# Seven block products for eight in the value product of batches 4 to 7, accumulated in one bank with copies between

## Chip, cores and metric

One Trainium2 chip, one core. The metric is device time of one launch in microseconds (us), median of several executions. Kernel before: 342.56 us (342.53 to 343.09), as it stood when the prediction was made. A profile is one such execution; its span is some 2 us shorter than the time (339.4 us for 341.31 in the profile of the kernel before, 338.8 for 340.82 in that after). The profile of the kernel before is of an execution of 341.31 us, so of one faster than that median.

## The reference

Eight batches, eight heads, 576 tokens, head size 64, all float32. Linear attention without softmax, RMS norm per head, then a gated linear unit with a causal convolution of five taps as gate:

```
kv   = einsum('bhsd,bhse->bhde', k, v)
out  = einsum('bhsd,bhde->bhse', q, kv)
x    = out / sqrt(mean(out*out, -1) + 1e-6) * g_norm        # then heads side by side: (B, S, 512)
gate = sigmoid(sum over k of conv_w[k] * shifted(x, k))     # five taps, causal
val  = x @ w_val                                            # 576x512 by 512x512, per batch
y    = (gate * val) @ w_out
```

## The kernel before

The kernel writes down "steps" with an engine, a duration and needs; a planner puts them into one program order, shifted by a table of hand-found offsets (SHIFTS). So each change to a step or a buffer gives all five engines a new order. The parts that matter:

```python
BANKS = {"kv": 1, "raw": 2, "tp": 2, "mm": 3}        # PSUM banks; tp = transposes, mm = products

def val_product(b, jt, n):            # 128 output columns, 288 tokens; 8 of these per batch
    val = ps("mm", [P, SV], f"val{b}_{jt}_{n}")
    for kc in range(NK):              # NK = 4 blocks of the inner dimension
        nc.tensor.matmul(val[:], wval[:, kc, jt * P:(jt + 1) * P],
                         xTs[b % 3][:, kc, HALO + n * SV:HALO + (n + 1) * SV],
                         start=(kc == 0), stop=(kc == NK - 1))

def keep_val(b, jt, n): nc.scalar.copy(out=gv[...], in_=st["val", b, jt, n][:])     # ScalarE
def gate_tap(b, jt, tap): nc.vector.scalar_tensor_tensor(...)                       # VectorE, 4 per gate
def gate_end(b, jt): nc.scalar.activation(out=gate[:], in_=gate[:], func=AF.Sigmoid)  # ScalarE
def gated(b, jt): nc.vector.tensor_tensor(out=both, in0=both, in1=gate[:], op=ALU.mult)
def halo(b): ...                      # GpSimd, edge tokens of xT; waits for DMAs that move xT
def powers(b, c): ...                 # GpSimd, mean square -> 1/rms ("rt")
...                                   # cut: loads, weight conversion, attention, the planner
```

The output product (w_out) already used seven block products for eight in this kernel.

## Time and profile before

| | before |
|---|---|
| time | 342.56 us |
| profiled span, mean granted TensorE clock | 339.4 us, 0.995 |
| TensorE (PE) busy | 315.1 us, 93% |
| VectorE (DVE) busy | 270.4 us, 80% |
| ScalarE (ACT), GpSimd (POOL) busy | 139.4, 140.0 us |
| TensorE instructions | 2161, of them value product 512 |

How to read it: TensorE sets the time from about 42 us on (busy for 270.3 of the 272 us from 42 to 314); the columns "idle before" and "releaser" of a group or of the timeline say what ended a wait. One more measure is used throughout, and I work it out from the timeline: the **lag** of TensorE at an instruction is its start time less the work that stands before it in TensorE's queue, each kind counted at its issue interval of the undisturbed middle (value 0.2427 us, fast output 0.2158, attention 0.1117, small key-value products 0.0365). Where the lag grows, TensorE lost time, by idling or by running slower; where it stays level, nothing was lost. The kernel before has a lag of 15.5 us at work 91, 16.1 at work 180, 16.1 at work 290 and 18.8 at its last product: it loses next to nothing between 110 and 315 us. (How transposes are weighted isn't given. Redone from the traces with transposes counted as attention, single values move by up to 0.8 us from work 90 on and by up to 3 us before it, but differences between kernels by 0.5 at most; it is the differences that count below.)

### The profile page before, as it was taken

The numbers are of one execution on the slowest core, as the hardware profiler recorded it, in microseconds if no ns is written. First come the engines' busy times: TensorE is split into PE (matmuls) and PEld (weight loads), VectorE is DVE, ScalarE is ACT, GpSimd is POOL, SyncE is SP. The second block draws the span as 40 slices with busy tenths as digits, with TensorE's granted clock in tenths as the row PEclk, the third lists the DMA queues.
The fourth block names the chain that finished last, engine by engine and source line by source line (L and its number), as shares of the span: only waits on it lengthen the run. The fifth ranks groups of instructions, "written<-read, shape, count | busy, mean of one in ns | idle before, by whom it ended". The sixth has DMA issues, their size and how long they took to land.

```text
span 339.4 us, 6185 instructions
## 1 busy us (share of the span) xinstructions
PE 315.1 (93%) x2161; PEld 254.7 (75%) x2161; DVE 270.4 (80%) x496; ACT 139.4 (41%) x293; POOL 140.0 (41%) x178
## 2 busy tenths in 40 slices
PE   0858999999999999999999999999999999999794
PEld 0747777878778877788778888778878876878681
DVE  4607999989999799896999899789956997297620
ACT  5528983873134253235134533172215322353010
POOL 3007314784356642683365585601717458000000
PEclk9998999999999999999999999999999999999999
DMA  6999979997077979787793165365333215220223
GB/s 165 287 329 306 320 219 299 250 315 168 3 178 196 244 233 280 187 236 207 206 256 86 32 154 157 71 182 144 79 89 85 64 31 129 58 63 2 62 62 93
DMA packets 46012, 55.35 MB, mean 163 GB/s; under 512 B 15754, under 2 KB 36254, under 8 KB 45982
## 3 DMA queue, kind: packets, MB, share of 16 engines
q1 hardware_dynamic: 42750, 48.67, 52.7%
q0 software_dynamic: 3072, 6.30, 8.3%
q8 instruction: 17, 0.28, 0.4%
q14 instruction: 13, 0.11, 0.1%
q10 hardware_dynamic: 160, 0.00, 0.0%
HBM read 39.21 MB, written 9.44 MB: 143 GB/s over the span
## 4 chain that ended last, share of the span: by engine, by line
PE 77%; DVE 8%; DMA 8%; ACT 3%; SPq 2%; issue 1%; POOL 1%; DVEq 0%
PE val L567 34%; PE ac L639 15%; PE b L639 11%; PE raw L469 8%; DMA q<-in_q_dram 5%; PE kv L392 4%; DMA k<-in_k_dram 2%; PE out L587 2%; PE qTps L430 2%; DVE gate L555 2%; PE xTps L515 1%; DVE sums L622 1%; DVE gv L580 1%; DMA out_dram<-ot 1%; DVE ss L491 1%
## 5 line engine op out<-in xcount | busy, mean ns | idle before, releaser
L567 PE MATMUL val<-xT,wval 128*128 128x288 f32 x512 | 129.5, 407 | 0.5 <-ACT gv L576 0.5
L567 PEld LDWEIGHTS val<-xT,wval 128*128 128x128 f32 x512 | 95.8, 190 | 26.9 <-issue 1.5
L497 POOL TENSOR_TENSOR rt<-ss,mhalf 128x8 f32<-128x8 f32 (+1 forms) x40 | 66.5, 1668 | 114.7 <-DVE ss L491 114.4
L555 DVE SCALAR_TENSOR_TENSOR gate<-xT,cwT,gate 128x576 f32<-128x576 f32 x128 | 97.4, 808 | 1.9 <-ACT gate L549 1.9
L538 POOL DMA_DIRECT2D xT<-y x96 | 52.9, 557 | 18.1 <-issue 6.5
L576 ACT COPY gv<-val 128x288 f32<-128x288 f32 x64 | 25.3, 395 | 69.3 <-PE val L567 69.1
L469 PEld LDWEIGHTS raw<-kvbd,qT 128*128 128x128 f32 (+1 forms) x320 | 36.8, 187 | 5.0 <-issue 1.9
L469 PE MATMUL raw<-kvbd,qT 128*128 128x128 f32 (+1 forms) x320 | 40.1, 286 | 0.0
L491 DVE TENSOR_REDUCE ss<-sq 128x8 f32<-128x520 f32 (+1 forms) x40 | 25.0, 630 | 17.5 <-ACT sq L483 17.5
L639 PE MATMUL b<-wsum,sums 128*128 128x256 f32 x128 | 33.6, 385 | 3.1 <-DVE sums L622 2.7
L639 PE MATMUL ac<-wout,gv 128*128 128x256 f32 x128 | 33.6, 385 | 0.2 <-DVE ot L662 0.2
L483 ACT ACTIVATE sq<-raw 128x512 f32<-128x512 f32 (+1 forms) x40 | 22.0, 553 | 24.0 <-PE raw L469 23.9
L639 PEld LDWEIGHTS b<-wsum,sums 128*128 128x128 f32 x128 | 23.1, 190 | 7.7 <-DVE sums L622 2.3
L504 DVE TENSOR_TENSOR x<-raw,rt 128x512 f32<-128x512 f32 (+1 forms) x40 | 24.9, 627 | 3.0 <-POOL rt L497 2.7
L639 PEld LDWEIGHTS ac<-wout,gv 128*128 128x128 f32 x128 | 23.4, 190 | 4.7 <-DVE ot L662 1.1
L562 ACT ACTIVATE gate<-gate 128x576 f32<-128x576 f32 x32 | 21.6, 684 | 11.8 <-DVE gate L555 11.4
L580 DVE TENSOR_TENSOR gv<-gv,gate 128x576 f32<-128x576 f32 x32 | 24.0, 749 | 2.6 <-ACT gv L576 1.9
L545 POOL COPY xT<-xT 128x124 f32<-128x124 f32 x32 | 18.7, 622 | 13.5 <-DMA xT<-y 13.5
L549 ACT ACTIVATE gate<-xT,cwT 128x576 f32<-128x576 f32 x32 | 22.2, 765 | 2.3 <-DMA xT<-y 2.2
L392 PEld LDWEIGHTS kv<-v,k 128*64 128x64 f32 x512 | 17.8, 138 | 6.5 <-issue 5.7
L392 PE MATMUL kv<-v,k 128*64 128x64 f32 x512 | 20.4, 225 | 1.9 <-DMA v<-in_v_dram 1.9
L655 ACT COPY ot<-ac 128x256 f32<-128x256 f32 x16 | 6.0, 372 | 35.6 <-PE ac L639 30.1
(78 smaller groups left out, 335.1 us busy)
## 6 DMA issues: line engine op xcount, KB each, us to landing
q<-in_q_dram SPq DMA_DIRECT2D x96, 140.0 KB, 4.6
out_dram<-ot SPq DMA_DIRECT2D x144, 64.0 KB, 1.8
k<-in_k_dram SPq DMA_DIRECT2D x16, 512.0 KB, 8.0
v<-in_v_dram SPq DMA_DIRECT2D x16, 512.0 KB, 7.3
xT<-y POOLq DMA_DIRECT2D x96, 64.0 KB, 2.7
w_wval<-in_moe_w_val_dram SPq DMA_DIRECT2D x4, 512.0 KB, 7.0
q<-in_q_dram SPq DMA_DIRECT2D x4, 512.0 KB, 8.7
w_wout<-in_moe_w_out_dram SPq DMA_DIRECT2D x4, 512.0 KB, 8.6
```

The lines of the kernel that those rows point to most:

```text
L392: nc.tensor.matmul(kvp[r * D:(r + 1) * D, hp, :], st["k", b, half][:, h, j, :] if j < NJ else kl[:, 2 * hp + r, :], st["v", b, half][:, h, ...
L469: nc.tensor.matmul(raw[row * m:(row + 1) * m, col * P:(col + 1) * P], st["qT", b][:, hp, c * P:c * P + m], kv_bd[b % 2][:, hp, :], start=T ...
L491: nc.vector.reduce_sum(out=ss[:, 0:n], in_=st["sq", b, c][:, 0:n], axis=AX.X)
L497: nc.gpsimd.tensor_tensor(out=rt[:, 0:n], in0=st["ss", b, c][:, 0:n], in1=mhalf[:, 0:n], op=ALU.pow)
L504: nc.vector.tensor_tensor(out=x[:, 0:n * D].rearrange("p (h e) -> p h e", h=n), in0=st["raw", b, c][:, 0:n * D].rearrange("p (h e) -> p h ...
L538: nc.gpsimd.dma_start(out=xTs[b % 3][i * TB:(i + 1) * TB, :, first:first + P], in_=y[a * TB:(a + 1) * TB, i])
L549: nc.scalar.activation(out=gate[:], in_=xTs[b % 3][:, jt, HALO:SX], func=AF.Copy, scale=cwT[:, K - 1, jt:jt + 1])
L555: nc.vector.scalar_tensor_tensor(out=gate[:], in0=xTs[b % 3][:, jt, tap * TB:tap * TB + S], scalar=cwT[:, tap, jt:jt + 1], in1=gate[:], op ...
L567: nc.tensor.matmul(val[:], wval[:, kc, jt * P:(jt + 1) * P], xTs[b % 3][:, kc, HALO + n * SV:HALO + (n + 1) * SV], start=(kc == 0), stop=( ...
L576: nc.scalar.copy(out=gv[:, jt, first:first + SV], in_=st["val", b, jt, n][:])
L580: nc.vector.tensor_tensor(out=both, in0=both, in1=st["gate", b, jt][:], op=ALU.mult)
L639: nc.tensor.matmul(st[bank, i, p], tokens()[:, k], weights_[:, k], start=(n < 2 and k == 0), stop=(k == NK // 2 - 1), skip_group_check=True)
```

## The change

Intent: per batch, the value product is a 2x2 block product; with sums of blocks of x and of w_val beforehand it needs 7 block products for 8. Block products pile up in one bank: product 0, 2, 4 and 6 go into bank "a" one onto the other, and between them ScalarE or VectorE copies the intermediate state out. The core of the diff:

```diff
-    BANKS = {"kv": 1, "raw": 2, "tp": 2, "mm": 3}
+    BANKS = {"kv": 1, "raw": 2, "tp": 1, "mm": 4}
+    FAST_VAL = range(4, B)
+    GATES = 3                       # gate buffers, were 4; xT buffers 2, were 3 (comments added here)
+    def val_sums(n): ...            # 4 sums of value weights, once          (VectorE)
+    def x_sums(b, n): ...           # 4 differences of x per batch           (VectorE)
+    def val_fast(b, mj, n):
+        bank, weights_, tokens = (
+            ("a", wval[:, EVEN, cols(0)], block(EVEN, 0)), ("c", vsum[:, 0, :, cols(0)], total(0)),
+            ("a", vsum[:, 1, :, cols(0)], total(1)), ("b", wval[:, ODD, cols(0)], block(ODD, 0)),
+            ("a", vsum[:, 2, :, cols(0)], total(2)), ("c", vsum[:, 3, :, cols(0)], block(ODD, 1)),
+            ("a", wval[:, ODD, cols(1)], total(3)))[n]
+        for k in range(NK // 2):
+            nc.tensor.matmul(st[bank, "val", b, mj][:], weights_[:, k], tokens()[:, k],
+                start=(n in (0, 1, 3) and k == 0), stop=(k == NK // 2 - 1), skip_group_check=True)
+    def val_keep(b, mj, n):         # n 0,1,2,6: ScalarE copies; 3,4,5: VectorE adds into gv
+        ...
+    def out_bank(i, p):             # the last output pairs use attention's banks
+        return "raw" if i == B // 2 - 1 and p != 2 else "mm"
     def fast_product(i, p, n):      # output product: same bank scheme, 3 adds and 4 copies per pair
...                                  # cut: gates in order 0,2,1,3; weight conversions in the
...                                  #      output buffers (ot); planner entries
-SHIFTS = {...}                      # all offsets new: loads, weight conversions, attention, gates
+SHIFTS = {...}
```

## The prediction

> **What bounds the kernel now.** I read the page first (busy shares, slices), then the groups, then the chain that ended last in order of time, then the start on VectorE.
>
> ```profile
> PE 315.1 (93%) x2161; PEld 254.7 (75%) x2161; DVE 270.4 (80%) x496; ACT 139.4 (41%) x293; POOL 140.0 (41%) x178
> ...
> PE   0858999999999999999999999999999999999794
> ...
> DVE  4607999989999799896999899789956997297620
> ...
> DMA  6999979997077979787793165365333215220223
> ```
>
> TensorE (PE) is idle for 24.3 of 339.4 us. Tables by stretch place it: 15.5 us before 42 us (loads and the first attention), 1.7 between 42 and 300, 1.9 at about 317, some 5 in the last copy and store. In the middle nothing but TensorE work sets the time, so an instruction removed there is worth its issue interval, if nothing new waits. The chain in order of time (start, length) gives the intervals, the groups (busy, mean ns) the durations of the other engines:
>
> ```profile
> 195.94 13.58 PE val L567 x56
> 209.53 0.86 PE ac L639 x4
> ```
>
> ```profile
> L567 PE MATMUL val<-xT,wval 128*128 128x288 f32 x512 | 129.5, 407 | 0.5 <-ACT gv L576 0.5
> ...
> L576 ACT COPY gv<-val 128x288 f32<-128x288 f32 x64 | 25.3, 395 | 69.3 <-PE val L567 69.1
> ...
> L580 DVE TENSOR_TENSOR gv<-gv,gate 128x576 f32<-128x576 f32 x32 | 24.0, 749 | 2.6 <-ACT gv L576 1.9
> ...
> L655 ACT COPY ot<-ac 128x256 f32<-128x256 f32 x16 | 6.0, 372 | 35.6 <-PE ac L639 30.1
> ...
> L662 DVE TENSOR_TENSOR ot<-b,ot 128x256 f32<-128x256 f32 x16 | 6.7, 418 | 1.8 <-PE b L639 1.6
> ...
> L606 DVE TENSOR_TENSOR wsum<-wout 128x512 f32<-128x512 f32 x2 | 1.4, 677 | 0.0
> ```
>
> A value matmul shows as two instructions; 56 take 13.58 us, 0.2425 each[...]. A product of the fast output (4 instructions) takes 0.86.
>
> [...] 407 ns busy against 242 issued. I count intervals, not busy time. [...]
>
> **The change, part by part.**
> 1. Removed: batches 4 to 7 need 7 block products of 4 instructions in each of 2 column pairs, 56 where 64 were. That is 32 instructions x 0.2425 = **7.8 us**. My count over the whole order of instructions, each kind at its interval, gives 315.4 before and 307.7 after.
> 2. VectorE: 16 differences of x at 0.75 (12.0), 24 block adds at about 0.45 (10.8, scaled from 0.418 for 256 columns), 4 weight sums at 0.68 (2.7); the re-ordered output products use 3 adds for 5, which saves 32 x 0.418 = 13.4. Net **+12 us**, to about 282. To see whether it becomes the bound I set the sums of VectorE work and TensorE work side by side at each point where a product needs a sum. Before, the second batch's sums came just in time (the products wait at 109 us, and 104 to 109 of the chain is VectorE). After, that place has 3 us more VectorE work ahead, but one weight block is converted in the idle gap at 14 to 25 us, so it is about level. In the last four batches VectorE leads by 10 to 14 us. So it should not become the bound, though its reserve at the end shrinks from 27 us to about 13.
> 3. ScalarE: 8 copies per batch as before, and 4 for 2 in each output pair, 32 more x 0.37 = 12. It ends near 45%, off the path except through waits.
> 4. New waits. After product 0, a copy must end before product 2 goes into the same bank, with product 1 between; so again from 2 to 4 and 4 to 6. The trace has a copy start 0.26 us after the product's last issue, lasting 0.395 (add 0.45), and TensorE following 0.06 later: 0.72 against 0.97 of product 1. That fits, with little left to load the weights early (0.19). Before, 18 such waits had just one product between and cost under 1 us together. After, by the order, there are 37, 17 of them in the value product. Whenever ScalarE is in a 0.77 us gate start or VectorE in a 0.75 us tap, one slips. I take 0.04 us each: **+1.5 us**. One bank change (batch 6's first half to the next output) has no work between: **+0.8**.
> 5. The tail, from the same chain:
>
> ```profile
> 316.26 0.41 ACT gv L576
> ...
> 316.69 0.77 DVE gv L580
> ...
> 317.48 0.70 DVE sums L622
> ...
> 318.21 0.70 DVE sums L622
> ...
> 318.96 1.13 PE b L639 x4
> ```
>
> TensorE waits 1.87 us for copy, gating and two sums. The new product order needs one sum first (0.7 less), and two output products now lie beside the copy and gating where one did. The path after the last value product is 0.28 + 0.40 + 0.76 + 0.69 + 0.07 = 2.2 us, against 1.7 of products: about 0.5 is left, a gain of **1.3**. Attention's banks spare the last pairs a wait for a free bank, but their second output buffer is still held by its store, as before (0.24). The last copy and store stay.
> 6. The start, where the order of loads and the banks change too (transposes have one bank for two). The timeline of TensorE, then of VectorE:
>
> ```profile
> 24.41 6.05 PE L469 MATMUL raw<-kvbd,qT 128*64 128x128 f32 x40
> ...
> 38.27 0.63 PE L515 MATMUL xTps<-ident,x 128*128 128x128 f32 x4
> ```
>
> ```profile
> 25.53 0.42 DVE L491 TENSOR_REDUCE ss<-sq 128x4 f32<-128x260 f32 x1 [11.22 <-ACT sq L483]
> 26.45 0.43 DVE L327 TENSOR_SCALAR wexp_wval<-w_wval 128x512 uint32<-128x512 uint32 x1 [0.49 <-DMA w_wval<-in_moe_w_val_dram]
> ```
>
> Transfers limit this stretch (DMA share over 1 from 6 us on; 6.8 MB by 26 us). After, a value weight block and the next batch's small q come ahead of the last half of v: 0.66 MB more, so the first attention product starts at about 25.5 for 24.4. Two converting steps for output weights stand in VectorE's queue before and among the first sums; their data are 6.6 and 7.1 MB down the queue, an estimated 27.7 and 29.2 us. [...] the last x is ready at about 39.5 for 38.05, and TensorE reaches that transpose with 19.8 us of work done, not 21.4. Together about **+2.9 us**. Since TensorE is then later and VectorE is not, the small VectorE waits between 42 and 110 us (1.2 us) should go: **-1.2**.
>
> Sum: -7.8 - 1.3 + 1.5 + 0.8 + 2.9 - 1.2 = -5.1, so **337.5 us**.
>
> **Rivals.**
> A: all of the removed time is gained and the start costs nothing. TensorE is saturated from 42 to 314 us, and the skeleton of loads is near the same. 342.6 - 7.8 - 1.3 + 1 = 334.5. Against it: the two weight conversions in front of the first sums.
> B: a new wait takes the place of the removed work. Each value product now depends on ScalarE and VectorE every 0.97 us, where the former product ran 1.94 us alone with three free banks. With 0.15 us lost at each of 37 tight waits (a third of a busy engine's usual remainder) that is 5.6, not 1.5: 341.5. For it: VectorE is over 90% busy there. Against it: 18 tight waits before cost almost nothing, and the order was plainly tuned anew around them.
> C: VectorE becomes the bound of the last batches (reserve used up by gates with 3 buffers for 4, x with 2 for 3). Each 0.76 us step of lag appears in full at the output products: 342 to 345. The reserve of 10 us or more speaks against it.
>
> **Range and chances.** The removal is certain, the start is the largest doubt (0 to +4), then the tight waits (0.5 to 5). 80%: 334.0 to 341.0. Faster by over 2% means under 335.7: it needs the start to cost under 1 us or so, which I give 0.31. Slower by 2% needs C and B together: 0.03.
>
> **What would show it.** Right: value instructions 480, not 512, still 0.242 apart; VectorE about 282 us busy; idle of TensorE before 42 us up by 2 to 4; gap at the last sums under 0.8 us; TensorE waits on copies 1 to 3 us in total. Start wrong: the first x transposes done at 38 us with idle still 15.5. B right: TensorE (or its weight load) idle on the copies to gv and ot by 4 us or more. C right: several us idle on x differences, sums or gating after 190 us, with VectorE over 95% busy. Above 341 or under 334 my account of the waits is wrong.

## The result, and the profile after

The changed kernel took **340.88 us** (340.60 to 341.98, 4 runs), the kernel before on the same chip 342.82 (342.53 to 343.25, 4 runs). Ratios here are the mean time of one kernel's fast runs over that of the other's of the same rounds, so not quite the ratio of the quoted medians: 0.9948, 95% interval 0.9923 to 0.9974. Half a per cent faster, inside the predicted range, but little over a third of the predicted gain (1.9 us of 5.1). A second set of executions on another chip (after_again, below) gave 0.9973, so the two estimates of the gain are 1.8 and 0.9 us.

The head of the page after, to be set against the line of before in the prediction:

```profile
PE 312.4 (92%) x2129; PEld 250.4 (74%) x2129; DVE 281.3 (83%) x504; ACT 151.2 (45%) x325; POOL 139.6 (41%) x178
```

32 TensorE instructions fewer, VectorE at 281.3 us (predicted 282), ScalarE 12 more: the counted parts came out as counted. Now the table by stretch, before and then after; columns are start and end, length, busy time of TensorE, weight load, VectorE, ScalarE and GpSimd (with instructions), granted TensorE clock, DMA share and GB/s:

```profile
0.00:42.00 42.00, 26.55 (x349) 22.94 (x350) 23.37 (x64) 25.73 (x58) 11.72 (x19) 0.96 1.03 281
42.00:110.00 68.00, 66.69 (x586) 54.14 (x583) 66.14 (x118) 35.52 (x75) 34.31 (x32) 1.00 0.75 204
...
190.00:250.00 60.00, 60.00 (x341) 47.67 (x339) 54.83 (x93) 22.15 (x45) 28.72 (x43) 1.00 0.48 122
250.00:300.00 50.00, 50.00 (x237) 40.24 (x234) 34.82 (x59) 18.57 (x38) 21.70 (x29) 1.00 0.29 72
```

```profile
0.00:42.00 42.00, 23.35 (x290) 19.97 (x291) 25.27 (x64) 24.33 (x52) 11.74 (x19) 0.94 1.04 287
42.00:110.00 68.00, 68.00 (x553) 55.25 (x551) 65.18 (x116) 37.48 (x80) 24.30 (x26) 0.99 0.83 218
...
190.00:250.00 60.00, 58.30 (x393) 45.42 (x392) 55.40 (x97) 22.69 (x50) 32.95 (x44) 1.00 0.52 133
250.00:300.00 50.00, 49.36 (x224) 38.87 (x223) 45.38 (x76) 21.27 (x46) 21.77 (x29) 1.00 0.27 64
```

TensorE is idle 3.2 us more before 42 us, 1.3 less up to 110 us, and has gaps from 190 to 300 us where it had none. VectorE was 97% busy from 42 to 110 us before already, and is 96% after.

The lag, point by point (same work, both profiles):

| at | before | after | what the step adds |
|---|---|---|---|
| work 90 (about 106 and 110 us) | 15.5 | 20.5 | start: +5.0 |
| work 180 | 16.1 | 20.4 | middle: -0.7 |
| work 290 | 16.1 | 24.7 | batches 4 to 7: +4.3 |
| last product | 18.8 | 26.0 | tail: -1.4 |

Together +7.2, against 7.8 us of work removed: -0.6, which is the difference of the two spans (339.4 and 338.8). The timed gain was 1.9. The gap comes from the profile of before: its execution took 341.31 us, 1.5 less than the median of the timed ones (342.82), while that of after, 340.82, lay at its median, and a second profile of the changed kernel (after_again) has the same lag at work 90. Time and granted clock go together: in the set of runs of the kernel before that stood beside after_again, 14 executions at 0.992 or more have a median span of 338.75 us, 20 at 0.985 or less 341.4, which is 2.65 us (0.8%) more and over the whole gain of this change. Which of the two brings about the other isn't shown. So 1 to 2 us of the start's 5.0 belong to the execution profiled, not to the kernel: 1.3, if the timed gain is taken as the true sum.

**The start.** VectorE after, where the first sums of squares (ss) wait behind a converting step for the output weight and its data:

```profile
27.41 0.43 DVE L330 TENSOR_SCALAR wexp_wout<-w_wout 128x512 uint32<-128x512 uint32 x1 [0.79 <-DMA w_wout<-in_moe_w_out_dram]
27.76 0.42 DVE L494 TENSOR_REDUCE ss<-sq 128x4 f32<-128x260 f32 x1
```

The first sum came at 27.76 for 25.53, 1.6 us after ScalarE had done its squares (sq, from 25.77 for 0.39 us): it stood behind the converting step, which waited 0.79 us for its data, until 27.41. TensorE in the same stretch, before and then after:

```profile
36.03 2.11 PE L567 MATMUL val<-xT,wval 128*128 128x288 f32 x8
...
40.83 0.64 PE L392 MATMUL kv<-v,k 128*64 128x64 f32 x16
```

```profile
29.98 0.66 PE L525 MATMUL xTps<-ident,x 128*128 128x128 f32 x2 [2.28 <-ACT sq L486]
30.43 1.92 PE L472 MATMUL raw<-kvbd,qT 128*128 128x128 f32 x8
...
38.97 0.66 PE L525 MATMUL xTps<-ident,x 128*128 128x128 f32 x4 [2.20 <-ACT xT L532]
39.56 0.69 PE L395 MATMUL kv<-v,k 128*64 128x64 f32 x16
40.07 0.38 PE L395 MATMUL kv<-vl,kl 128*64 128x64 f32 x4
40.23 1.07 PE L395 MATMUL kv<-v,k 128*64 128x64 f32 x16
```

Two things are to be seen. A transposition of x stands ahead of ready attention work in TensorE's queue and waits 2.28 us; another waits 2.20 us for the one transpose bank. And after each wait the same instructions take longer in this profile: 8 attention instructions (at 30.43 us) 1.92 us for 1.06, 16 key-value products (at 40.23 us) 1.07 us for 0.64, the first 8 value instructions (at 42.36 us) 2.69 for 2.11. The granted clock was 0.74 from 28 to 32 us and 0.57 from 40 to 44 us in this execution; in the one profiled for after_again, with waits of 2.28 and 2.31 us at the same places, it was 1.00 and 0.73. In the kernel before it was 0.64 from 24 to 28 us, after a wait of 1.89 us. What sets it isn't shown.

**The late batches.** The largest stall, at 216 us, read downwards through four engines (GpSimd, VectorE, ScalarE, TensorE):

```profile
211.06 1.16 POOL L555 COPY xT<-xT 128x124 f32<-128x124 f32 x4 [5.72 <-DMA xT<-y]
212.20 1.03 POOL L500 TENSOR_TENSOR rt<-ss,mhalf 128x4 f32<-128x4 f32 x1
```

```profile
213.26 0.42 DVE L515 TENSOR_TENSOR x<-raw,rt 128x256 f32<-128x256 f32 x1 [1.89 <-POOL rt L500]
213.61 1.54 DVE L565 SCALAR_TENSOR_TENSOR gate<-xT,cwT,gate 128x576 f32<-128x576 f32 x2
```

```profile
215.18 0.68 ACT L572 ACTIVATE gate<-gate 128x576 f32<-128x576 f32 x1 [2.01 <-DVE gate L565]
215.77 0.35 ACT L723 COPY ot<-cb 128x256 f32<-128x256 f32 x1
```

```profile
216.18 1.13 PE L710 MATMUL cb<-wout,gv 128*128 128x256 f32 x4 [1.47 <-ACT ot L723]
...
276.80 1.13 PE L710 MATMUL cb<-wout,gv 128*128 128x256 f32 x4 [0.42 <-ACT ot L723]
278.95 1.13 PE L710 MATMUL cb<-wout,sums 128*128 128x256 f32 x4 [0.16 <-DVE ot L719]
```

GpSimd's halo of batch 5 waits for a DMA (5.72 us), the powers of batch 6 stand behind it, VectorE's normalising waits for them (1.89 us), gate taps of batch 4 stand behind that, ScalarE's sigmoid waits for the taps (2.01 us), the copy of a finished bank stands behind the sigmoid, and TensorE waits for the copy (1.47 us). The product that is copied at 215.77 had ended at 213.6. The lag rises by 1.4 there, 0.4 at 230.8, 0.6 at 276.8 and 0.3 at 279.0 us: 2.7 of 4.3; the rest comes in steps of 0.1 to 0.2, mostly where one kind of product follows another. All four are waits of an output product for the copy or addition that must come between two products in one bank.

The tail is as predicted: the wait at the last sums is short.

```profile
318.18 1.13 PE L710 MATMUL cb<-wsum,sums 128*128 128x256 f32 x4 [0.28 <-DVE sums L687]
```

### The profile page after: what moved, and what is told of

The parts are those of the page before. It is cut to its first block, busy times and chain, and to the rows that moved or that the text cites. A ratio compares the mean times of both kernels' runs of the same rounds, so it can differ in the third digit from the quotient of the medians.

```text
span 338.8 us, 6161 instructions
## 1 busy us (share of the span) xinstructions
PE 312.4 (92%) x2129; PEld 250.4 (74%) x2129; DVE 281.3 (83%) x504; ACT 151.2 (45%) x325; POOL 139.6 (41%) x178
## 4 chain that ended last, share of the span: by engine, by line
PE 69%; DMA 10%; DVE 10%; SPq 4%; issue 3%; ACT 2%; DVEq 0%
PE val L577 19%; PE a L710 12%; PE cb L710 11%; PE raw L472 7%; PE va L627 6%; DMA q<-in_q_dram 6%; PE kv L395 5%; PE vc L627 3%; DMA w_wout<-in_moe_w_out_dram 2%; SPq L739 2%; PE out L655 2%; PE qTps L433 2%; DVE gate L565 2%; DVE ot L719 2%; DMA kl<-in_k_dram 1%
## 5 line engine op out<-in xcount | busy, mean ns | idle before, releaser
L500 POOL TENSOR_TENSOR rt<-ss,mhalf 128x8 f32<-128x8 f32 (+1 forms) x40 | 68.2, 1706 | 109.4 <-DVE ss L494 109.2
L577 PE MATMUL val<-xT,wval 128*128 128x288 f32 x256 | 65.7, 410 | 0.0
L577 PEld LDWEIGHTS val<-xT,wval 128*128 128x128 f32 x256 | 48.2, 192 | 12.6 <-issue 0.3
L710 PE MATMUL a<-wsum,sums 128*128 128x256 f32 x128 | 33.3, 382 | 0.0
L494 DVE TENSOR_REDUCE ss<-sq 128x8 f32<-128x520 f32 (+1 forms) x40 | 25.2, 631 | 4.4 <-ACT sq L486 4.1
L719 DVE TENSOR_TENSOR ot<-cb,ot 128x256 f32<-128x256 f32 x32 | 13.4, 418 | 16.7 <-PE cb L710 8.0
L515 DVE TENSOR_TENSOR x<-raw,rt 128x512 f32<-128x512 f32 (+1 forms) x40 | 24.7, 620 | 2.5 <-POOL rt L500 2.5
L586 ACT COPY gv<-val 128x288 f32<-128x288 f32 x32 | 12.7, 400 | 30.8 <-PE val L577 30.8
L710 PEld LDWEIGHTS a<-wsum,sums 128*128 128x128 f32 x128 | 23.4, 190 | 3.3
L555 POOL COPY xT<-xT 128x124 f32<-128x124 f32 x32 | 16.4, 553 | 7.0 <-DMA xT<-y 5.9
L433 PE MATMUL qTps<-ident,q 128*64 128x128 f32 (+1 forms) x160 | 13.3, 319 | 6.5 <-DMA q<-in_q_dram 4.9
L710 PE MATMUL cb<-wout,gv 128*128 128x256 f32 x64 | 16.6, 382 | 1.9 <-ACT ot L723 1.9
```

The lines of the kernel that those rows point to most:

```text
L494: nc.vector.reduce_sum(out=ss[:, 0:n], in_=st["sq", b, c][:, 0:n], axis=AX.X)
L500: nc.gpsimd.tensor_tensor(out=rt[:, 0:n], in0=st["ss", b, c][:, 0:n], in1=mhalf[:, 0:n], op=ALU.pow)
L515: nc.vector.tensor_tensor(out=x[:, 0:n * D].rearrange("p (h e) -> p h e", h=n), in0=st["raw", b, c][:, 0:n * D].rearrange("p (h e) -> p h ...
L577: nc.tensor.matmul(val[:], wval[:, kc, jt * P:(jt + 1) * P], xTs[b % 2][:, kc, HALO + n * SV:HALO + (n + 1) * SV], start=(kc == 0), stop=( ...
L710: nc.tensor.matmul(st[bank, i, p], tokens()[:, k], weights_[:, k], start=(n < 2 and k == 0), stop=(k == NK // 2 - 1), skip_group_check=True)
```

## The experiments

Fifteen kernels ran, in four groups, each group on one chip beside the kernel before (341.3 to 342.4 us there, scattering by 4 to 5 us). Ratios are to the kernel before, from fast executions alone, with their 95% interval; times are medians of all.

### plain_val: eight products again, all else as changed

```diff
-    FAST_VAL = range(4, B)
+    FAST_VAL = range(B, B)
```

> The changed kernel with 8 value products again in batches 4 to 7 (nothing else undone); the order of instructions is the same up to 188 us. It adds 7.8 us of TensorE work after 188 us and takes 23 us of VectorE work and 32 copies between products away. Theory W (the new waits on VectorE and ScalarE in the last four batches cost about 4.4 us, as the lag of TensorE behind its work grew from 20.4 to 24.9 us between 206 and 310 us): 340.9 + 7.8 - 4.4 = 344.3. Rival H (all that is missing was lost in the start, the seven products gain their whole 7.8): 348.7.

Correct, 351.07 us, ratio 1.0256 (1.0212 to 1.0299): some 10 us over the changed kernel, above both theories and more than the 7.8 of the products: in this order there is also a wait of 3.61 us on VectorE before 263 us. So it doesn't say what the seven products are worth, nor does it part the costs.

### nowait_val: the copies between products wait for nothing

Result wrong on purpose: the copies after products 0, 1, 2 and the add after 4 read a weight in SBUF in place of the bank, so TensorE need not wait for them.

```diff
-            nc.scalar.copy(out=to(0, 0), in_=a)
+            nc.scalar.copy(out=to(0, 0), in_=other)      # other = wout[:, mj, 0:SV]; likewise n = 1, 2, 4
```

> Wrong result on purpose, same order of instructions: the copies after value products 0, 1, 2 and the add after 4 read a weight from SBUF and not the bank, so TensorE never waits for a copy between value products. Rival B (the tight waits inside the value product are the cost): 336.5 to 337.5. Theory V (the cost sits where VectorE is late, and shows at output products): 1 us or less gained, 339.9 to 340.9.

340.85 us, ratio 0.9975 (0.9953 to 0.9996), and the lag grows by 4.1 us from work 180 to 260, in the changed kernel by 4.3; TensorE's idle time from 190 to 300 us is 2.5 us (changed kernel 2.3). The time lies with the changed kernel's 0.9948 and 0.9973. The tight waits of the value product (copies of 0.40 us and adds of 0.45 between products of 0.97) cost nothing measurable. That takes away 17 of the 37 waits that the prediction had counted, not the 20 of the output product.

### short_taps: less VectorE work in the late gates

Result wrong on purpose: the gate taps of batches 4 to 7 on a quarter of the columns.

```diff
+        w = S // 4 if b in FAST_VAL else S
-            out=gate[:], in0=xTs[b % 2][:, jt, tap * TB:tap * TB + S],
+            out=gate[:, 0:w], in0=xTs[b % 2][:, jt, tap * TB:tap * TB + w],
```

> Wrong result on purpose, same order: the 64 taps of the gates of batches 4 to 7 run over a quarter of the columns, which takes about 64 x 0.45 = 29 us off VectorE and leaves every wait in place. Theory V (VectorE late in the last four batches, ScalarE's gate ends and the copies behind them with it): TensorE's stalls after 206 us go, 336.5 to 338. Rival B (tight waits themselves): within 1 us of 340.9.

The 0.45 us per tap is an estimate from the trace of the kernel before: a VectorE product or sum of two tensors takes 0.749 us over 576 columns (gv, L580) and 0.418 over 256 (ot, L662), so in proportion 432 columns fewer are worth about 0.45. 338.57 us, ratio 0.9901 (0.9863 to 0.9940). The product of the stall at 216:

```profile
215.21 1.13 PE L711 MATMUL cb<-wout,gv 128*128 128x256 f32 x4 [0.36 <-ACT ot L724]
```

There the lag steps up by 0.3 us for 1.4, at 277 to 279 by nothing over 0.3, and the lag grows by 1.8 from work 180 to 260 where it grew by 4.3. TensorE's idle time from 190 to 300 us falls from 2.3 to 0.7. So the larger part of the late loss came by way of VectorE being late.

### late_order: six steps put later, same work

Each step is taken out of the finished program order and put in again behind another (written short here):

```diff
+MOVES = [((halo, 5), after (powers, 6, 4)),
+    ((gate_end, 4, 1), after (fast_keep, 1, 3, 2)), ((gated, 4, 1), after (gate_end, 4, 1)),
+    ((gate_end, 6, 0), after (fast_keep, 2, 3, 1)), ((gate_end, 6, 2), after (fast_keep, 2, 3, 2)),
+    ((gated, 6, 2), after (fast_keep, 2, 3, 4))]
```

> The changed kernel with six steps of the batches 4 to 7 put later in the queues and nothing else: GpSimd's halo of batch 5 after the powers of batch 6, ScalarE's sigmoid of gates of batches 4 and 6 after the output copies that TensorE waits for. Queue theory: the stalls of TensorE at 216 (1.4 us) and at 277 to 279 us (0.9 together) go or shrink to 0.4 or less, the lag grows from work 180 to 300 by 2.5 to 3.5 us instead of 5, and the time falls by 0.4 to 0.7% against after_again. Rival (VectorE as a whole is short of time there, so that what is put later is missed later): the stall at 216 goes but returns at the next gating or output copy, lag at work 300 within 0.7 us of after_again's, time within 0.2%.

Correct, 339.36 us, ratio 0.9906 (0.9882 to 0.9930); the unaltered changed kernel beside it (after_again, below) 0.9973. GpSimd and TensorE in the place of the chain above:

```profile
210.02 1.47 POOL L510 TENSOR_TENSOR rt<-ss,mhalf 128x4 f32<-128x4 f32 x1 [1.84 <-DVE ss L504]
214.15 2.04 POOL L565 COPY xT<-xT 128x124 f32<-128x124 f32 x4 [2.65 <-DMA xT<-y]
```

```profile
217.16 0.38 PE L535 MATMUL xTps<-ident,x 128*128 128x128 f32 x2
217.38 1.03 PE L720 MATMUL cb<-wout,gv 128*128 128x256 f32 x4
```

The product follows at once. The lag grows by 3.2 us from work 180 to 300 (after_again 5.0), and TensorE's idle time from 190 to 300 us is 0.7 (after_again 2.1). VectorE has as much to do as before (281.2 us busy in this profile, 281.3 in the changed kernel's), so it was not short of time there: steps stood in the wrong place. Of the six, one is GpSimd's, three are ScalarE's and two VectorE's; they were moved together, so it isn't shown which of them won how much.

### after_again, two_tp, late_two: the yardstick, and the second transpose bank

> The changed kernel itself, unaltered, as the yardstick for the runs beside it. Both theories (the lost gain went into queue order in the start and late; or it is contention that differs from chip to chip) expect a time near the first one, 0.995 of the kernel before. If it comes out under 0.990 or over 1.000, the chip decides more than the queues do and small ratios of other runs can only be read against this one. In the profile: lag of TensorE (start time minus work standing before it) of about 21.5 us at work 21, 22 to 23 at work 200, near 26 at the last product; a stall of 1.4 to 1.7 us at about 216 us.

340.88 on the first chip, here 341.60 us, ratio 0.9973 (0.9948 to 0.9997); lag 20.4 at work 90, the same stalls. Five of its 22 executions (344.6 to 346.0 us, clock 0.980 or less) count as slow and are left out of the ratio, none of the 56 of the kernel before; with all of them the means would be equal (342.4 and 342.3 us). In its start the first attention product after the wait of 2.28 us ran at its usual pace (1.92 us in the first profile of the changed kernel):

```profile
30.34 1.06 PE L472 MATMUL raw<-kvbd,qT 128*128 128x128 f32 x8
```

```diff
-    BANKS = {"kv": 1, "raw": 2, "tp": 1, "mm": 4}
+    BANKS = {"kv": 1, "raw": 2, "tp": 2, "mm": 3}
```

> Same order, correct result: transposes get two PSUM banks and the products three (in place of one and four). Theory T (one bank for the transposes delays the start): the first value product, at 42.4 us after the change and 36.0 before, starts 2 to 4 us earlier, and the time falls by 2 or so, less what three product banks cost later. Rival L (loads and weight conversions ahead of the first sums in VectorE's queue): the first value product starts at most 1 us earlier.

two_tp: 340.67 us, ratio 0.9977 (0.9953 to 1.0000). Its profile has a lag of 17.9 at work 90, 2.6 less than the changed kernel's, but the times show no gain. Here a single profile misled me: it is of the fastest of the 20 executions (339.15 us).

> The changed kernel with the six later steps of late_order and two transpose banks (three for products) in place of one and four. Theory (start and late batches add up): late_order took 2.2 us off the changed kernel's time (0.9906 for 0.9973); the second bank lowered the lag at work 90 by 2.6 us in its profile but the time by 1 us or less: expected ratio to the kernel before 0.984 to 0.989, about 337. Rival (what is won in the start is lost again in the late batches, as TensorE then comes too early for VectorE): 0.990 or more.

late_two (late_order with two banks): 338.63 us, ratio 0.9890 (0.9853 to 0.9927), lag 19.5 at work 90; by time it stands at the border of the two theories. Against late_order's 0.9906 the second bank is worth 0.5 us, within the noise. I lay no weight on it.

### before_one_tp: the single bank in the kernel before

```diff
-    BANKS = {"kv": 1, "raw": 2, "tp": 2, "mm": 3}
+    BANKS = {"kv": 1, "raw": 2, "tp": 1, "mm": 3}
```

> The kernel before with one PSUM bank for transposes in place of two, its order and everything else unaltered. Theory T1: the single bank by itself costs the start, since each transposed block must be copied out before the next is turned; then the lag at the first value product and after grows by 1.5 to 2.5 us over that of the kernel before (16.5 to 18.5 or more at work 42) and the time by 0.5 to 0.7%. Rival T2: the single bank costs only together with the new order, in which the copies out of it stand on ScalarE behind steps of a weight conversion; then under 0.7 us is added.

354.14 us, ratio 1.0335 (1.0276 to 1.0395), lag 25.2 at work 21 and 29.7 at 42. In the old order one bank costs over 11 us, far above either theory. A likely reason, not tested, is that transposes of q and x alternate all through the start there. The order of the changed kernel was made for one bank. Bank and order can't be judged apart.

### head_order: ten steps of the start put later

```diff
+MOVES = [((narrow_weight, wout, 3, 0), after (normalise, 0, 4)), ...     # and its ScalarE steps 1 to 3
+    ((narrow_weight, wout, 1, 0), after (sums, 0, 3)),
+    ((narrow_weight, wval, 2, 1), after (keep_x, 0, 2)), ...             # and steps 2 to 4
+    ((turn_x, 0, 4), after (raw_product, 0, 1))]
```

> The changed kernel, one transpose bank as it has, with ten steps of the start put later in the queues and nothing else: the output weight's first conversion steps (VectorE and ScalarE) after the first x, the second one after the second sums, the last value weight's ScalarE steps after the copies of transposed x, and the first transposition of x after the next attention product. Queue theory: the steps that wait for data or for another engine stood ahead of ready work; the lag at the first value product falls by 2 to 3.5 us (21.7 to 18.2-19.7), the first value product starts at 39 to 40.5 instead of 42.4, and the time falls by 0.6 to 1.0% against after_again. Rival (loads and the bank set the start): the lag falls by less than 1 us and the time by under 0.3%.

341.50 us, ratio 0.9974 (0.9949 to 0.9999), no gain on after_again: the rival's figure. Its profiled execution was a slow one (clock 0.975, 0.50 to 0.55 from 32 to 44 us), so its lag is not compared. But its TensorE shows that the waits were moved and not removed:

```profile
29.77 0.41 PE L539 MATMUL xTps<-ident,x 128*128 128x128 f32 x2 [0.46 <-DVE x L529]
33.16 1.98 PE L447 MATMUL qTps<-ident,q 128*64 128x128 f32 x16 [2.98 <-ACT xT L546]
```

The wait of 2.28 us has become one of 0.46, and the next transposition waits 2.98 us for the one bank, whose copy stands behind weight conversions on ScalarE. So this run doesn't tell what the start would be without these waits.

### old_start, old_start_late: the start in the order of the kernel before

Two banks, the first 134 steps in the old order, sums of value weights put off to batch 2; the second with the moves of late_order.

```diff
+START = [...]        # names of the first 134 steps of the kernel before, one load left out
+steps = [those of START, in its order] + [all others, in the changed kernel's order]
+MOVES = [((val_sums, 0), after (normalise, 2, 0)), ...]
```

> The changed kernel with two transpose banks, whose first 134 steps (loads, weight conversions, first attention, up to the last transposed x of batch 0) stand in the order of the kernel before, and whose sums of value weights are put off to batch 2; everything after in the changed kernel's order. Theory (the start's order and bank cost some 4.7 us of lag and the rest of the kernel keeps that): lag at work 42 about 16.5 to 17.5 us (kernel before 16.5, changed kernel 21.6), time 3.5 to 5 us under the changed kernel, ratio 0.982 to 0.988. Rival (VectorE is the bound between 42 and 110 us if TensorE starts early, since it has 3 us more to do): the lag rises again by 2 to 4 us before work 110, TensorE waits there on sums or gating, ratio 0.990 to 0.996.

> old_start with the six later steps of late_order: both causes undone, seven products for eight kept. Theory: the full sum of the prediction without start and late waits, lag 17 at work 42 and 19 to 20 at work 300, ratio 0.973 to 0.980 (333 to 336 us), faster than both kernels by over 2%. Rival as for old_start: a wait on VectorE takes back 2 us or more, 0.983 to 0.990.

old_start 344.39 us, ratio 1.0088 (1.0056 to 1.0120); old_start_late 342.06 us, 1.0017 (0.9993 to 1.0041). TensorE of old_start:

```profile
35.17 2.11 PE L721 MATMUL val<-xT,wval 128*128 128x288 f32 x8
...
52.44 3.13 PE L616 MATMUL raw<-kvbd,qT 128*64 128x128 f32 x16 [5.88 <-ACT qT L603]
```

ScalarE before the copy of q that ends this wait:

```profile
49.76 1.28 ACT L716 ACT_TABLE_LOAD   x1
51.39 0.68 ACT L716 ACTIVATE gate<-gate 128x576 f32<-128x576 f32 x1 [0.35 <-DVE gate L709]
51.98 0.66 ACT L603 COPY qT<-qTps 128x280 f32<-128x280 f32 x2
```

The start is as early as wanted: first value product at 35.17, lag 15.0 at work 27. Then it is lost, most of it in one wait of 5.88 us: the copies of q that TensorE needs stand on ScalarE behind weight conversions, a table load of 1.28 us and a sigmoid, and this one waited 0.35 us for gate taps on VectorE. The rest goes as TensorE runs slowly after the wait (the 16 attention instructions take 3.13 us, usually 1.95; the granted clock was 0.79 from 44 to 60 us). The lag is 23.1 at work 90. Both theories had expected a gain. So the old start joined to the new rest is worse; it doesn't tell whether VectorE has too much work there or the seam is badly ordered. The late moves gave 0.7% here too.

### before_extra and short_vsums: VectorE's work in the first 110 us

before_extra: the kernel before with four more additions on VectorE where the changed kernel sums its weights.

```diff
+            if at in (("normalise", 0, 0), ("gate_tap", 0, 1, 0)):
+                for _ in range(2):
+                    nc.vector.tensor_tensor(out=wsum[:, 0], in0=wval[:, 0:2, 0:256], in1=wval[:, 2:4, 0:256], op=ALU.add)
```

> The kernel before with four more additions on VectorE (128x512, about 0.61 us apart, 2.4 us in all, their result overwritten later), two after the last x of batch 0 and two after a gate tap of batch 0, where the changed kernel sums its value weights. Theory (VectorE is the second bound of the first 110 us, so that what is added to it there moves TensorE): lag of TensorE at work 91 rises from 15.5 by 1.5 to 2.5 us, time 0.4 to 0.7% longer. Rival (VectorE had room there; only the order of loads and the transposes' bank set the changed kernel's start): lag and time within 0.7 us, 0.2%.

343.10 us, ratio 1.0055 (1.0032 to 1.0078), 1.9 us for 2.4 us of work; lag 17.1 at work 91 for 15.5. TensorE of before, then of before_extra, at the same instruction:

```profile
50.99 1.16 PE L469 MATMUL raw<-kvbd,qT 128*128 128x128 f32 x8
```

```profile
52.58 1.16 PE L469 MATMUL raw<-kvbd,qT 128*128 128x128 f32 x8 [1.63 <-DVE x L504]
```

VectorE is a second bound of the kernel before in its first 110 us: what is added to it there in this order moves TensorE by most of its length (1.6 of 2.4 us in the lag).

short_vsums: late_two with the four weight sums on 32 of 256 columns (wrong on purpose).

```diff
-        nc.vector.tensor_tensor(out=vsum[:, n], in0=one, in1=two, op=op)
+        nc.vector.tensor_tensor(out=vsum[:, n, :, few], in0=one[:, :, few], in1=two[:, :, few], op=op)
```

> late_two with the four sums of value weights on 32 of 256 columns (result WRONG on purpose), 1.7 us less of VectorE before work 90. If VectorE sets TensorE's place there: lag at work 90 falls by 1 to 1.7 us (19.5 in late_two), ratio to the kernel before 0.984 to 0.986 (late_two 0.989). If the head's order sets it: no change within 0.5 us, 0.989.

338.61 us, ratio 0.9894 (0.9856 to 0.9932): no change against late_two (0.9890), with VectorE busy for 271.9 us from 12 to 340 us in the profile, late_two 273.6. In late_two these sums are not what TensorE waits for. My reading of the two runs, not shown by either alone: before, VectorE had no reserve; after, TensorE comes later and VectorE has some.

### tuned_order, tuned_order2: another order of all the same work

Same instructions, two banks; every engine's queue reordered by moving single steps in a list-scheduling model, from old_start_late and from late_two on.

```diff
-        for step in plan.order():
+        for step in [by_at[int(n)] for n in TUNED.split()]:
```

> The changed kernel's steps with two transpose banks in a wholly new order of each engine's queue, found by moving single steps in a list-scheduling model from old_start_late on; same instructions, same arithmetic. Theory (the lost gain is a matter of queue order in the start and in batches 4 to 7, not of the work): lag 15.5 to 17.5 at work 40 and 16.5 to 18.5 at work 240, no stall over 0.5 us from 50 to 310 us, ratio 0.972 to 0.982, faster than all before it. Rival (VectorE has too much work before 110 us for any order): lag at work 90 stays at 19 to 21, ratio 0.985 to 0.995.

> As tuned_order, but found from late_two on, so the changed kernel's start with fewer alterations. Theory: lag 17 to 19.5 at work 40 and about the same at 240, ratio 0.976 to 0.986. Rival: as late_two, 0.989 or more.

Both correct: 336.97 us, ratio 0.9852 (0.9804 to 0.9899), and 336.92 us, 0.9862 (0.9823 to 0.9901). The table by stretch of tuned_order2, to be set against the two above:

```profile
0.00:42.00 42.00, 26.06 (x351) 22.94 (x353) 22.42 (x60) 24.37 (x58) 12.06 (x19) 0.96 1.01 283
42.00:110.00 68.00, 67.36 (x558) 54.43 (x555) 64.54 (x113) 36.70 (x77) 28.86 (x27) 1.00 0.93 251
...
190.00:250.00 60.00, 59.19 (x379) 46.65 (x378) 56.03 (x97) 24.12 (x55) 29.91 (x41) 1.00 0.32 79
```

Before 42 us TensorE does nearly what it did in the kernel before (26.06 us busy, 26.55 then). The lag is 17.8 at work 90 and 21.2 at work 290. These are the fastest kernels of the study, 1.4% ahead of the kernel before, but at or beyond the slow end of what was expected of them (0.972 to 0.982, and 0.976 to 0.986), and their intervals overlap those of late_two (0.9890) and short_vsums (0.9894). With such an order the changed kernel is nearly as far ahead as I had predicted (4.9 us of 5.1). The kernel before was not searched in the same way, so it is not shown how much of this it could have had too.

## Why the prediction was wrong

Taken in the order of its sum:

1. **-7.8 for 32 value instructions: right.** 480 remain, still 0.97 us per product of four.
2. **-1.3 for the tail: right.** 1.4 in the lag; the gap is 0.28 us.
3. **VectorE +12 to about 282 us: right** (281.3).
4. **+1.5 and +0.8 in batches 4 to 7: the step that failed, in size and in cause.** The prediction put the cost down to 37 tight waits of 0.04 us and a bank change; 4.3 us were lost there. nowait_val shows that the tight waits of the value product cost nothing. I did not take away those of the output product alone, and the four stalls found are all of these: few and long, up to 1.4 us, and not many and short. The largest two are waits for a copy that stood behind a sigmoid that waited for VectorE (short_taps, late_order). This is rival C's engine with another mechanism: it was put aside because "VectorE leads by 10 to 14 us" in sums of work. VectorE did have the time; late_order wins about 2 us with its work unchanged. What the sums hide is where in the queue a wait falls. That TensorE's idle time from 190 to 300 us alone, 2.3 us, equals the predicted sum is luck: it comes from four waits, and 2 us more went without idling, in products that followed more slowly. For the 0.8 no stall of its own is seen.
5. **+2.9 - 1.2 at the start: mis-sized.** The idle time alone is what was predicted: +3.2 before 42 us (predicted 2 to 4), -1.3 up to 110 us. But the lag at work 90 rose by 5.0, some 3.7 if the fast profile of before is allowed for. The missing term is TensorE running slowly: in the profile after, the listed key-value, value and attention instructions take up to 1.8 times their usual time. The kernel before pays it too (its first 40 attention instructions 6.05 us, at the usual interval 4.5), so the difference is an estimated 1.4 us by the durations in the two timelines. By the same reckoning some 1.2 us more are lost before 20 us (16 transposes of q at 16.07 us take 1.97 us, later 1.09). In after_again the slow running falls in other places (none at 30 us, more before 22), about 2 us in all over the kernel before, and the lag is the same. Idle time and slow running together so make up most of the 5.0; before has only one profile to compare with.
6. **The whole.** -7.8 - 1.4 - 0.7 + 3.7 + 4.3 = -1.9, as timed; the 3.7 is fitted to that and no check of it. All the signs that the prediction had named for being right came true (480 value instructions, VectorE 281.3, idle +3.2, last gap 0.28, waits on copies 2.3 us), and still little over a third of the gain was there: the signs count idle time, and part of the loss is none.

Rival B's time (341.5) was nearest, with a reason that holds at four output products and not at the 37 tight waits. Rival A fell by the start and the late waits together.

What stays open is how the start's loss divides between order, transpose bank and VectorE. No single correction gave it back (two_tp, head_order, old_start, short_vsums); before_extra shows VectorE as a bound of the old order; only orders that move both engines together (tuned_order, tuned_order2) seem to have won some of it: by the lag of tuned_order2 (17.8 at work 90), while in time their lead over late_two is within the intervals. And these changed everything at once.

## What to carry to other kernels

Reserve in sums of work says that an engine can keep up, not that it will: in the traces here ScalarE and VectorE took their queues in order (the copy at 215.77 us, whose product had ended at 213.6, started behind the sigmoid at 215.18, which had waited 2.01 us for VectorE; the sum at 27.76, whose squares were done at 26.16, behind a converting step that waited 0.79 us for its data). So follow what stands ahead of each instruction that the bound engine waits for, through every engine, and put steps that wait for a DMA or another engine behind those that are due. When a change takes buffers and gives the planner a new order, count the new order as part of the change, and test it alone by reordering the same work. Judge the start by many executions, since single profiles were off by 1.5 us here (that of before and that of two_tp), and look at the granted clock beside the time.
